# Weight maxima over the partitions through a small tensor in memory instead of TensorE

## The chip, the cores and the metric

The kernel runs on one core of one Trainium2 chip. The metric is the device time of one execution in microseconds, and of several executions the median. The engines are called by the profile's short names in its rows: PE (TensorE), PEld (its weight loads), DVE (the vector engine), ACT (the scalar engine), POOL (GpSimd) and SP (the engine that issues most transfers).

## The reference

A linear attention (RWKV) gives tokens x (3072 × 384). A mixture of 8 experts follows, in which every token goes through every expert, weighted by a matrix that Sinkhorn steps have balanced:

```python
logits = x @ w_gate;  P = np.exp(logits - logits.max())
for _ in range(8):
    P /= P.sum(1, keepdims=True) + 1e-09
    P /= P.sum(0, keepdims=True) + 1e-09
    P *= N / E
for e in range(E):                      # w1: 8 x 384 x 1024, w2: 8 x 1024 x 384
    h = np.maximum(x @ w1[e], 0.0)
    out += P[:, e:e + 1] * (h @ w2[e])
```

All of it is float32. The kernel keeps that accuracy by splitting each float32 operand into a high and a low float16 part and making three float16 matmuls of each product (high by high, high by low, low by high). For the weights this needs a scale: a power of two, found from the largest absolute value of w1 and of w2 in the part at hand. That maximum is over all 128 partitions, and every partition needs it.

## The kernel before, in words

**First part.** The attention runs in 24 chunks, with expert 0's layers interleaved. What is left of expert 0 then runs beside the Sinkhorn steps and the preparation of stage 0's weights.

**Stages.** Experts 1 to 7 are done in 14 stages (`NS`), each half of an expert's hidden dimension (512 of 1024). A stage has 60 slots: two halves of the tokens (g), two column halves (j), and 15 products (n) each. So slots 0 to 14 are g = 0, j = 0; slots 15 to 29 are g = 0, j = 1; slots 30 to 59 are g = 1. In the loop at lines 1135 to 1150 each slot puts out three things, in this order: one product of the first layer (`g1_slots`), three matmuls of 512 columns on TensorE; then the tasks that a table has put on this slot; then 4 or 5 matmuls of 384 columns (5, 5, 5, 5, 4) of the second layer (`g2_tiles`) of the token half before. In stage 0 the token half before belongs to expert 0 and has only a remainder, which is used up in the first half of the 30 slots of g = 0; after it those slots hold first-layer matmuls alone.

**First layer.** A scheme with 15 products in place of 18 computes the layer from sums of weight blocks (made by GpSimd in the preparation) and sums of token blocks. The products go into five chains, each in a PSUM bank of its own: A, Y, Z, C and B (tiles bA, bY, ...). `ORDER` and `CHAIN` (lines 614 to 617) say which product goes on which chain. `after(n)` (line 960) has the vector and the scalar engine read the chains as they grow: `vadd` combines a bank with a temporary in the buffer `tb` (t0, t1, t2, t4, s2), and `keep` makes the two float16 parts of the hidden values, high on the scalar engine, low on the vector engine. A chain's bank is read while the chain is still to be added to, so a later product on it waits for that read; and banks go round, so a new chain waits until the last reader of the bank's old chain is done. Banks come from two pools: every third chain takes one of 2 banks (`ph`), the others one of 4 (`pq`).

**Second layer.** A tile of 128 tokens takes 12 matmuls into one of two PSUM banks (`po`). The scalar engine multiplies by the gate into one of three staging buffers (`stg`), and the tile is added to `accd` in memory, by transfers that GpSimd issues (in stage 0 they are plain stores on SP).

**Preparation of the next stage's weights** (`stage_weights`, line 768; put on slots in `stage_tasks`, line 1088). In slot 0 SP loads raw w1 and w2 into `rawb` (128 × 3072). `amax` (slots 9, 10, 17, 18) takes four column maxima, each over 768 elements a partition, on the vector engine (tiles `wms`). `reduce_max` (slot 19) makes two of them, one for w1 and one for w2 (`wmas`). `across` (slot 21) starts the maximum over the partitions, `over_partitions` (line 134): TensorE transposes the 128 × 2 maxima into a PSUM bank, the vector engine takes the maximum of each row (`mt_s`) and puts the two on the diagonal of a 2 × 2 matrix (`md_s`). `scale` (slot 23) lets TensorE multiply that by ones, which gives both maxima on every partition, and `pow2_scale` (line 126) makes the scale of it in three small operations on the vector engine (`isw` twice, `sw`). The bank for this comes from the pool of 4, after stage 0's own. From slot 30 on the scalar engine (`high`) and the vector engine (`low`) convert the weights by that scale.

**Other tasks.** From stage 2 on, expert 0's results are added in: in slots 8, 23, 38 and 53 SP fetches two pieces (`hb<-e0d`), nine slots later they are summed on the vector engine, then weighted on the scalar engine and added to `accd` by GpSimd. SP takes its transfers in the order in which they were put out and waits at each for what it needs.

Of the kernel before, what the change touches and what calls it, by code (L numbers as in the profile page):

```python
# [8 lines left out]
F32 = mybir.dt.float32  # L9
# [3 lines left out]
ALU = mybir.AluOpType  # L13
AX = mybir.AxisListType
# [18 lines left out]
def rwkv_sinkhorn_moe(  # L33
# [13 lines left out]
    V, S_, G, T, Q = (  # L47
        InOrder(tc, e) for e in (nc.vector, nc.scalar, nc.gpsimd, nc.tensor, nc.sync)
    )
# [3 lines left out]
    E, _, F = w1.shape  # L53
    P = 128
# [6 lines left out]
    TB = 512  # L61
# [10 lines left out]
    sm = ctx.enter_context(tc.tile_pool(name="sm", bufs=2))  # L72
# [41 lines left out]
        return v_[:, :, t % TH, :]  # L114

    accd = dram.tile([NT, DM], F32, name="accd")
    e0d = [dram.tile([NT, DM], F32, name=f"e0d{j}") for j in range(2)]
    logits = const.tile([P, NTT, E], F32, name="logits")
    inv_s = const.tile([P, NTT], F32, name="inv_s")
# [6 lines left out]
    def pow2_scale(m, inv, s, down):  # L126
        V.tensor_scalar(inv, m, 1e-30, down, op0=ALU.max, op1=ALU.mult)
        V.tensor_single_scalar(
            inv.bitcast(I32), inv.bitcast(I32), EXP_MASK, op=ALU.bitwise_and
        )  # L130
        V.reciprocal(s, inv)


    def over_partitions(m, n, pool, tag, name):

        pt = pool.tile([P, TB], F32, tag=tag, name=f"pmax_{name}")
        T.transpose(pt[:n, :P], m, ident)
        mt = sm.tile([P, 1], F32, tag="mt", name=f"mt_{name}")
        V.tensor_reduce(mt[:n], pt[:n, :P], axis=AX.X, op=ALU.max)
        md = sm.tile([P, 2], F32, tag="md", name=f"md_{name}")  # L140
        V.tensor_scalar_mul(md[:n, :n], ident[:n, :n], mt[:n])
        yield pt[:, 2 * P : 2 * P + n]
        T.matmul(pt[:, 2 * P : 2 * P + n], ones[:n, :], md[:n, :n], start=True, stop=True)
        yield pt[:, 2 * P : 2 * P + n]
# [617 lines left out]
    tb_ = big.tile([P, 13 * TS], F32, name="tb")  # L762
# [5 lines left out]
    def stage_weights(s):  # L768
        e, half = 1 + s // 2, s % 2
        home = ws0 if s % 2 == 0 else ws1  # L770
        w1s = part(home, F16, 0, (NPR, 2, TS))
        w2s = part(home, F16, NPR * 2 * TS, (2, FHC, DM))
        isw = sm.tile([P, 2], F32, tag="isw", name=f"isw_{s}", bufs=3)
        sw = sm.tile([P, 2], F32, tag="sw", name=f"sw_{s}")
        m = sm.tile([P, 4], F32, tag="wm", name=f"wms_{s}")
        ma = sm.tile([P, 2], F32, tag="wma", name=f"wmas_{s}")
        uc = part(ucb, F32, 0, (11, TS))

        def load():
            fs = slice(half * FH, (half + 1) * FH)  # L780
            Q.dma_start(raw1, w1[e][:, fs].rearrange("(c p) f -> p c f", p=P))
            Q.dma_start(raw2, w2[e][fs, :].rearrange("(c p) d -> p c d", p=P))

        def amax(i):
            n = KC * FH // 2
            V.tensor_reduce(
                m[:, i : i + 1], rawb[:, i * n : (i + 1) * n],
                axis=AX.X, op=ALU.max, apply_absolute_value=True,
            )

        res = []

        def reduce_max():
            V.tensor_reduce(ma, m.rearrange("p (j i) -> p j i", i=2), axis=AX.X, op=ALU.max)

        def across():
            res.append(over_partitions(ma, 2, *small(), f"s{s}"))
            next(res[0])

        def scale():  # L800
            pow2_scale(next(res[0]), isw, sw, 0.25)

        a = [raw1[:, i % KC, (i // KC) * TS : (i // KC + 1) * TS] for i in range(6)]
        u_ = {r_: uc[:, UI[r_]] for r_ in US[:11]}
        pool = [
            add(u_[0], a[0], a[2]), sub(u_[7], a[3], a[0]), add(u_[1], u_[7], a[4]),
            sub(u_[2], u_[1], a[1]), sub(u_[10], a[2], a[1]), add(u_[3], u_[2], u_[0]),
            sub(u_[8], a[5], u_[10]), add(u_[9], a[3], a[5]), sub(u_[12], a[4], u_[8]),
            sub(u_[13], a[2], a[5]), add(u_[14], a[0], a[5]),
        ]  # L810
        pieces = [
            (w1s[:, i : i + n], uc[:, i : i + n], 0) for i, n in ((0, 3), (3, 3), (6, 3), (9, 2))
        ] + [
            (w1s[:, 11:13], raw1[:, 0:2, :TS], 0), (w1s[:, 13:15], raw1[:, 1:3, TS:], 0)
        ] + [
            (w2s[:, :, i : i + 2].rearrange("p l c d -> p c l d"), raw2[:, i : i + 2], 1) for i in (0, 2)
        ]

        def high(i):
            o, x_, j = pieces[i]  # L820
            S_.activation(o[:, :, 0], x_, AF.Copy, scale=sw[:, j : j + 1])

        def low(i):
            o, x_, j = pieces[i]
            V.scalar_tensor_tensor(
                o[:, :, 1], x_, sw[:, j : j + 1], o[:, :, 0], op0=ALU.mult, op1=ALU.subtract
            )

        return dict(w1s=w1s, w2s=w2s, isw=isw, load=load, amax=amax, reduce_max=reduce_max, across=across,
                    scale=scale, pool=pool, high=high, low=low, n=len(pieces))  # L830

# [38 lines left out]

    def at(t, *fs):
        ticks.setdefault(t, []).extend(fs)

    small_ = [(ps2, "po")]

    def small():
        return small_[0]

    WS = {0: stage_weights(0)}
    sk = sinkhorn()  # L880
# [207 lines left out]
    def stage_tasks(s):  # L1088
        ts = {}

        def at(t, *fs):
            ts.setdefault(t, []).extend(fs)

        def gate():
            pes[s] = gate_of(1 + s // 2, WS[s]["isw"], s)

        at(2, gate)
        if s == 0:
            at(3, gate0)
        if s + 1 < NS:  # L1100
            w_ = WS[s + 1] = stage_weights(s + 1)
            at(0, w_["load"])
            for i, t in enumerate((9, 10, 17, 18)):
                at(t, lambda i=i: w_["amax"](i))
            for i, f in enumerate(w_["pool"]):
                at(8 + i, f)
            at(19, w_["reduce_max"])
            at(21, w_["across"])
            at(23, w_["scale"])
            for i, (th_, tl) in zip(  # L1110
                (4, 6, 0, 7, 1, 5, 2, 3),
                ((0, 2), (1, 3), (8, 9), (8, 10), (15, 17), (16, 18), (23, 24), (23, 25)),
            ):
                at(NSLOT + th_, lambda i=i: w_["high"](i))
                at(NSLOT + tl, lambda i=i: w_["low"](i))
        else:
            for _ in range(2 * FHC):
                at(20, load_final)
        for n in range(4):
            n4 = (s - 2) * 4 + n  # L1120
            if 0 < n4 <= NTT:
                at(15 * n + 2, flush(n4 - 1)[1])
                at(15 * n + 3, flush(n4 - 1)[2])
            if 0 <= n4 < NTT:
                at(15 * n + 8, flush(n4)[0])
        return ts
# [4 lines left out]

    rest = e0_rest()
    late = None
    small_[0] = (ps4, "pq")
    for s in range(NS):
        tasks = stage_tasks(s)
        for g in range(NG):
# [43 lines left out]
```

## Time and profile before

| | |
|---|---|
| median of 3 runs | 1607.49 us (1604.43, 1607.49, 1607.59) |
| the profiled execution's own time | 1602.74 us |
| its span, first to last instruction | 1601.0 us |
| mean granted TensorE clock | 0.995 |
| busy: PE, DVE, ACT, POOL | 98%, 64%, 42%, 37% of the span |
| first layer: one matmul of a chain, 840 each on bY and bZ | mean 379 ns, overlapping |
| second layer: one matmul into po, 3360 with hbx | mean 326 ns, overlapping |

All rows are of one profiled execution. A row of the groups reads: source line, engine, operation, out<-in by the program's names, shapes, count, then the busy time in us and the mean of one in ns, then the idle time of the engine just before and what ended it. A row of the sequence in time reads: start and duration in us, engine, operation, count, and in brackets the idle time before it and its releaser. Most instructions have line 29, a helper's, so tiles tell them apart. Matmuls are pipelined: a matmul's duration holds its way through the array, and the next one starts earlier than it ends.

### The profile page before, as it was taken

The numbers are of one execution on the slowest core, as the hardware profiler recorded it, in microseconds if no ns is written. First come the engines' busy times: TensorE is split into PE (matmuls) and PEld (weight loads), VectorE is DVE, ScalarE is ACT, GpSimd is POOL, SyncE is SP. The second block draws the span as 40 slices with busy tenths as digits, with TensorE's granted clock in tenths as the row PEclk, the third lists the DMA queues.
The fourth block names the chain that finished last, engine by engine and source line by source line (L and its number), as shares of the span: only waits on it lengthen the run. The fifth ranks groups of instructions, "written<-read, shape, count | busy, mean of one in ns | idle before, by whom it ended". The sixth has DMA issues, their size and how long they took to land.

```text
span 1601.0 us, 24304 instructions
## 1 busy us (share of the span) xinstructions
PE 1571.7 (98%) x9433; PEld 909.6 (57%) x9433; DVE 1019.0 (64%) x1706; ACT 668.6 (42%) x1190; POOL 587.9 (37%) x688
## 2 busy tenths in 40 slices
PE   7999999999999999999999999999999999999999
PEld 5778777555455555555555555555555555555555
DVE  6776665675766666666666666666665666656554
ACT  2333333343444444454535454544444453535320
POOL 6567674442021343434243424243332424242200
PEclk8999999999999999999999999999999999999999
DMA  7333230212022567566666656664545554545434
GB/s 180 63 69 85 66 86 26 92 42 84 35 94 54 104 85 124 74 123 85 124 84 100 110 74 123 85 113 55 95 55 94 58 96 54 94 56 89 60 89 133
DMA packets 163899, 136.60 MB, mean 85 GB/s; under 512 B 88257, under 2 KB 158018, under 8 KB 163778
## 3 DMA queue, kind: packets, MB, share of 16 engines
q0 software_dynamic: 44928, 61.36, 31.6%
q1 hardware_dynamic: 118640, 73.63, 15.9%
q8 instruction: 75, 1.23, 0.3%
q14 instruction: 46, 0.38, 0.1%
q10 hardware_dynamic: 210, 0.00, 0.0%
HBM read 53.69 MB, written 80.22 MB: 84 GB/s over the span
## 4 chain that ended last, share of the span: by engine, by line
PE 93%; DVE 3%; POOL 1%; issue 1%; ACT 1%; ACTq 0%; DVEq 0%; POOLq 0%
PE po L29 46%; PE bZ L29 11%; PE bY L29 11%; PE ph L29 5%; PE bB L29 4%; PE bA L29 4%; PE py L29 4%; PE bC L29 2%; PE pA L29 1%; PE pu L29 1%; POOL tb L29 1%; PE pz L29 1%; PE prT L29 1%; PE pkT L29 1%; PE px L29 0%
## 5 line engine op out<-in xcount | busy, mean ns | idle before, releaser
L29 PE MATMUL po<-ws,hbx 128*128 128x384 f16 x3360 | 736.9, 326 | 0.0
L29 POOL DMA_DIRECT2D accd<-stg x288 | 250.4, 870 | 701.2 <-ACT stg L29 682.8
L29 PEld LDWEIGHTS <-hbx 128*128 128x128 f16 x3576 | 336.9, 98 | 287.4
L29 PEld LDWEIGHTS <-ws 128*128 128x128 f16 x3096 | 302.8, 98 | 248.2 <-issue 6.3
L29 ACT ACTIVATE hbx<-tb 128x512 f16<-128x512 f32 x224 | 141.5, 632 | 443.5 <-DVE tb L29 443.5
L29 PE MATMUL po<-ws,hb 128*128 128x384 f16 x1248 | 322.2, 327 | 3.2 <-DVE ws L29 2.3
L29 DVE TENSOR_TENSOR tb<-bY,tb 128x512 f32<-128x512 f32 x168 | 116.2, 692 | 194.4 <-PE bY L29 193.3
L29 ACT ACTIVATE stg<-po,pe 128x384 f32<-128x384 f32 x312 | 179.6, 575 | 128.0 <-PE po L29 102.5
L29 PE MATMUL bZ<-xv,ws 128*128 128x512 f16 x840 | 227.0, 379 | 0.7 <-DVE tb L29 0.6
L29 PE MATMUL bY<-xv,ws 128*128 128x512 f16 x840 | 227.0, 379 | 0.1
L29 DVE TENSOR_TENSOR tb<-bZ,tb 128x512 f32<-128x512 f32 x168 | 115.5, 688 | 132.9 <-PE bZ L29 132.9
L29 PEld LDWEIGHTS <-hb 128*128 128x128 f16 x1248 | 122.1, 98 | 96.4 <-issue 4.7
L29 POOL TENSOR_TENSOR ucb<-rawb 128x256 f32<-128x256 f32 x84 | 75.5, 949 | 93.1 <-DMA rawb<-in_moe_w_dram 66.7
L29 DVE TENSOR_TENSOR tb<-bB,tb 128x512 f32<-128x512 f32 x112 | 77.5, 692 | 49.6 <-PE bB L29 47.7
L29 PE MATMUL ph<-hbx,ws 128*128 128x384 f16 x576 | 103.9, 328 | 1.3 <-DVE hb L29 1.2
L29 DVE SCALAR_TENSOR_TENSOR hbx<-tb,hbx 128x512 f16<-128x512 f32 x112 | 78.0, 696 | 24.3 <-ACT hbx L29 19.5
L29 DVE SCALAR_TENSOR_TENSOR hb<-tb,hbx 128x512 f16<-128x512 f32 x112 | 77.2, 689 | 24.7 <-ACT hbx L29 19.5
L29 PE MATMUL bA<-xv,ws 128*128 128x512 f16 x336 | 90.8, 379 | 1.0 <-ACT tb L29 1.0
L29 PE MATMUL bB<-xv,ws 128*128 128x512 f16 x336 | 90.8, 379 | 0.0
L29 DVE SCALAR_TENSOR_TENSOR hb<-ph,hb 128x384 f16<-128x384 f32 x64 | 35.5, 555 | 59.0 <-ACT hb L29 58.8
L29 ACT COPY tb<-bZ 128x512 f32<-128x512 f32 x56 | 32.8, 586 | 68.1 <-PE bZ L29 68.1
L29 ACT ACTIVATE hb<-ph 128x384 f16<-128x384 f32 x64 | 31.5, 492 | 58.0 <-PE ph L29 56.7
(163 smaller groups left out, 1645.0 us busy)
## 6 DMA issues: line engine op xcount, KB each, us to landing
accd<-stg POOLq DMA_DIRECT2D x288, 192.0 KB, 3.7
rawb<-in_moe_w_dram SPq DMA_DIRECT2D x28, 768.0 KB, 7.3
e0d<-stg SPq DMA_DIRECT2D x48, 192.0 KB, 1.9
hb<-e0d SPq DMA_DIRECT2D x48, 192.0 KB, 3.5
rn<-in_r_dram SPq DMA_DIRECT2D x24, 192.0 KB, 3.1
kn<-in_k_dram SPq DMA_DIRECT2D x24, 192.0 KB, 3.5
vn<-in_v_dram SPq DMA_DIRECT2D x24, 192.0 KB, 2.8
accd<-stg SPq DMA_DIRECT2D x24, 192.0 KB, 1.8
```

Source lines behind the costliest of these rows:

```text
L29: return lambda *a, **k: self.tc.keep_in_program_order(f(*a, **k))
```

## The change

It concerns the maxima over the partitions in the preparations for stages 1 to 13; stage 0's own preparation stays on TensorE. The vector engine's two maxima for each partition (128 × 2) are written to a small tensor in memory, `wmx`, and read back with all 256 values onto every partition, into columns of the buffer `tb` that the stages do not use otherwise. There one reduction on the vector engine gives both maxima, which `pow2_scale` takes as before. The column maxima stand in slots 9, 10, 11 and 15 (before: 9, 10, 17, 18), the two-column maximum and the write in slot 15 (before: 19), the reading back in slot 21, and the reduction with the scale in slot 29 (before: 23).

```diff
+    wmx = dram.tile([2 * E, P, 2], F32, name="wmx")
...
+        mb = tb_[:, 5 * TB : 5 * TB + 2 * P]
 
         def reduce_max():
             V.tensor_reduce(ma, m.rearrange("p (j i) -> p j i", i=2), axis=AX.X, op=ALU.max)
+            if s:
+                Q.dma_start(wmx[s], ma)
 
         def across():
-            res.append(over_partitions(ma, 2, *small(), f"s{s}"))
-            next(res[0])
+            if s:
+                Q.dma_start(
+                    mb, wmx[s].rearrange("(o p) j -> o (p j)", o=1).broadcast_to([P, 2 * P])
+                )
+            else:
+                res.append(over_partitions(ma, 2, ps2, "po", f"s{s}"))
+                next(res[0])
 
         def scale():
-            pow2_scale(next(res[0]), isw, sw, 0.25)
+            if s:
+                mj = sm.tile([P, 2], F32, tag="wmj", name=f"wmj_{s}")
+                V.tensor_reduce(mj, mb.rearrange("p (q j) -> p j q", j=2), axis=AX.X, op=ALU.max)
+            else:
+                mj = next(res[0])
+            pow2_scale(mj, isw, sw, 0.25)
...
-            for i, t in enumerate((9, 10, 17, 18)):
+            for i, t in enumerate((9, 10, 11, 15)):
                 at(t, lambda i=i: w_["amax"](i))
...
-            at(19, w_["reduce_max"])
+            at(15, w_["reduce_max"])
             at(21, w_["across"])
-            at(23, w_["scale"])
+            at(29, w_["scale"])
```

How the instructions move is shown for stage 2, which prepares stage 3's weights.

TensorE in slot 21, before. `bC` is the product of this slot, `pmax_s` the bank of the transpose, `po` the second layer:

```order
L29 MATMUL bC_0_1_9402<-xv_76,ws_74 128x512
L29 LDWEIGHTS ws_74
L29 MATMUL bC_0_1_9402<-xv_76,ws_74 128x512
L29 MATMUL pmax_s_9408<-ident,wmas_9137 2x128
L29 LDWEIGHTS hb_73
L29 MATMUL po_13_9396<-ws_75,hb_73 128x384
L29 LDWEIGHTS hbx
```

And now:

```order
L29 MATMUL bC_0_1_9398<-xv_76,ws_74 128x512
L29 LDWEIGHTS ws_74
L29 MATMUL bC_0_1_9398<-xv_76,ws_74 128x512
L29 LDWEIGHTS hb_73
L29 MATMUL po_13_9392<-ws_75,hb_73 128x384
L29 LDWEIGHTS hbx
```

The transpose is gone, and the second layer follows the first directly. The matmul by ones, after the products of slot 23, is gone in the same way.

The vector engine from slot 14 to slot 19, before. `wms` are the column maxima, `wmas` the two-column maximum, `hb<-hb` the sum of expert 0's pieces, the rows with b and a letter the adds on chains:

```order
L29 TENSOR_TENSOR tb<-bB_0_0_9247,tb 128x512
L29 SCALAR_TENSOR_TENSOR hbx<-bZ_0_0_9162,hbx 128x512
L29 SCALAR_TENSOR_TENSOR hbx<-tb,hbx 128x512
L29 TENSOR_TENSOR tb<-bY_0_1_9337,tb 128x512
L29 TENSOR_REDUCE wms_9136<-rawb 128x1
L29 TENSOR_TENSOR hb_73<-hb_73 128x384
L29 TENSOR_REDUCE wms_9136<-rawb 128x1
L29 TENSOR_TENSOR tb<-bY_0_1_9337,tb 128x512
L29 TENSOR_TENSOR tb<-bA_0_1_9324,tb 128x512
L29 TENSOR_REDUCE wmas_9137<-wms_9136 128x2
```

And now, from slot 11 to slot 16:

```order
L29 TENSOR_TENSOR tb<-bZ_0_0_9157,tb 128x512
L29 TENSOR_TENSOR tb<-bB_0_0_9242,tb 128x512
L29 TENSOR_REDUCE wms_9131<-rawb 128x1
L29 SCALAR_TENSOR_TENSOR hbx<-tb,hbx 128x512
L29 SCALAR_TENSOR_TENSOR hbx<-bY_0_0_9147,hbx 128x512
L29 TENSOR_TENSOR tb<-bB_0_0_9242,tb 128x512
L29 SCALAR_TENSOR_TENSOR hbx<-bZ_0_0_9157,hbx 128x512
L29 SCALAR_TENSOR_TENSOR hbx<-tb,hbx 128x512
L29 TENSOR_REDUCE wms_9131<-rawb 128x1
L29 TENSOR_REDUCE wmas_9132<-wms_9131 128x2
L29 TENSOR_TENSOR tb<-bY_0_1_9336,tb 128x512
```

One column maximum stands behind the two adds of slot 11; the other, with the two-column maximum, stands ahead of slot 16's add on chain Y.

The vector engine in slots 21 to 23, before. `mt_s` and `md_s` are the steps between TensorE's two, `isw` and `sw` the scale:

```order
L29 TENSOR_REDUCE mt_s_9410<-pmax_s_9408 2x1
L29 TENSOR_SCALAR md_s_9412<-ident,mt_s_9410 2x2
L29 TENSOR_TENSOR tb<-bY_0_1_9337,tb 128x512
L29 SCALAR_TENSOR_TENSOR hbx<-tb,hbx 128x512
L29 TENSOR_TENSOR tb<-bZ_0_1_9348,tb 128x512
L29 TENSOR_SCALAR isw_9134<-pmax_s_9408 128x2
L29 TENSOR_SCALAR isw_9134<-isw_9134 128x2
L29 RECIPROCAL sw_9135<-isw_9134 128x2
```

And now the steps stand in slot 29, between the operations of its own chain and the add of slot 31 (last row):

```order
L29 TENSOR_TENSOR tb<-bB_0_1_9435,tb 128x512
L29 SCALAR_TENSOR_TENSOR hbx<-bZ_0_1_9347,hbx 128x512
L29 TENSOR_REDUCE wmj_9497<-tb 128x2
L29 TENSOR_SCALAR isw_9129<-wmj_9497 128x2
L29 TENSOR_SCALAR isw_9129<-isw_9129 128x2
L29 RECIPROCAL sw_9130<-isw_9129 128x2
L29 SCALAR_TENSOR_TENSOR hbx<-tb,hbx 128x512
L29 TENSOR_TENSOR tb<-bY_1_0_9522,tb 128x512
```

`mt_s` and `md_s` have gone; the reduction of the values read back (`wmj`) and the three operations of the scale follow slot 29's adds, ahead of the last low part of that slot. On SP the write and the reading back stand next to each other, between the fetches of slots 8 and 23. On the scalar engine and on GpSimd the order is as before.

More of the change, by code (lines that the diff above doesn't have):

```diff
@@ L872, in at @@
         ticks.setdefault(t, []).extend(fs)
-    small_ = [(ps2, "po")]
-    def small():
-        return small_[0]
     WS = {0: stage_weights(0)}
@@ L1133, in rwkv_sinkhorn_moe @@
     late = None
-    small_[0] = (ps4, "pq")
     for s in range(NS):
```

## The prediction

> **What bounds the kernel now.** I read the head of the page and its chain of waits first, then a table by stretches, then TensorE's own sequence around the step that the change takes off it.
>
> ```profile
> span 1601.0 us, 24304 instructions
> PE 1571.7 (98%) x9433; PEld 909.6 (57%) x9433; DVE 1019.0 (64%) x1706; ACT 668.6 (42%) x1190; POOL 587.9 (37%) x688
> ...
> PE 93%; DVE 3%; POOL 1%; issue 1%; ACT 1%; ACTq 0%; DVEq 0%; POOLq 0%
> ```
>
> TensorE (PE) is busy for 98% of the span and carries 93% of the chain that ended last. But busy time of pipelined matmuls is no proof that an engine never waits, so the stretches come next: for each, the busy time of PE, PEld, DVE, ACT and POOL.
>
> ```profile
> 400.00:484.00 84.00, 81.91 (x437) 42.62 (x437) 57.95 (x91) 36.95 (x66) 8.62 (x11) 1.00 0.18 64
> 484.00:570.00 86.00, 86.00 (x472) 45.98 (x471) 54.56 (x85) 39.24 (x70) 25.39 (x31) 1.00 0.46 79
> 570.00:656.00 86.00, 86.00 (x472) 45.98 (x471) 55.94 (x88) 40.78 (x72) 32.26 (x39) 1.00 0.64 101
> 1432.00:1518.00 86.00, 86.00 (x472) 45.98 (x471) 49.92 (x79) 38.63 (x69) 20.80 (x24) 1.00 0.53 74
> ```
>
> From 484 us to 1518 TensorE has no idle time, at a granted clock of 1.00, in stage after stage (first, second and last shown); the vector engine is at 65% there (55.94 of 86). Whatever leaves TensorE's stream in those stages shortens the span, and whatever the change adds elsewhere is free while it fits between TensorE's due times. Before 484 us TensorE does wait: 2.1 us of the 84 from 400 on.
>
> Now one maximum over partitions in such a stage, on TensorE (start, us, then the instruction):
>
> ```profile
> 484.08 0.81 PE L29 MATMUL bC<-xv,ws 128*128 128x512 f16 x3
> 484.72 0.27 PE L29 MATMUL pmax_s<-ident,wmas 128*2 128x128 f32 x1
> 484.83 0.33 PE L29 MATMUL po<-ws,hb 128*128 128x384 f16 x1
> ...
> 487.11 0.81 PE L29 MATMUL bZ<-xv,ws 128*128 128x512 f16 x3
> 487.85 0.38 PE L29 MATMUL pmax_s<-md_s,ones 2*128 2x2 f32 x2
> 488.16 0.50 PE L29 MATMUL po<-ws,hbx 128*128 128x384 f16 x2
> ...
> 488.98 0.81 PE L29 MATMUL bB<-xv,ws 128*128 128x512 f16 x3
> 489.63 0.33 PE L29 MATMUL po<-ws,hb 128*128 128x384 f16 x1
> ```
>
> Starts, not durations, tell the cost, since durations overlap. Three matmuls of 512 columns with nothing behind them take 489.63 − 488.98 = 0.65 us. With the matmul by ones behind them they take 488.16 − 487.11 = 1.05, so it costs 0.40 us. The transpose costs 484.83 − 484.72 = 0.11.
>
> **The change part by part.**
>
> *TensorE loses the transpose and the matmul by ones in 13 of 14 weight preparations.* The count is in the groups by line:
>
> ```profile
> L29 PE MATMUL pmax_s<-md_s,ones 2*128 2x2 f32 x28 | 5.3, 256 | 0.8 <-DVE md_s L29 0.8
> ```
>
> Two rows for each (the product in float32 is done in two passes), so 14 preparations; the first (for stage 0) keeps its own. Of the 13, twelve lie in stages where TensorE never idles: 12 × (0.40 + 0.11) = **6.1 us**. A page's rule beside it: the Trainium skill, "TensorE: Matmul & The Clock Gate", section "Back-to-back issue gap", gives 134 cycles for 128 columns and about 25 ns for very small ones, an estimate of 0.11 us for the three instructions, and 1.3 us in place of 6.1 for twelve. The rows show 0.51 and have the last word.
>
> *The thirteenth (made in stage 0, for stage 1) stands where TensorE waits for the vector engine:*
>
> ```profile
> 402.25 0.81 PE L29 MATMUL bC<-xv,ws 128*128 128x512 f16 x3
> 404.06 0.27 PE L29 MATMUL pmax_s<-ident,wmas 128*2 128x128 f32 x1 [1.01 <-DVE wmas L29]
> 404.17 0.81 PE L29 MATMUL bY<-xv,ws 128*128 128x512 f16 x3
> 404.82 0.81 PE L29 MATMUL bZ<-xv,ws 128*128 128x512 f16 x3
> 406.42 0.38 PE L29 MATMUL pmax_s<-md_s,ones 2*128 2x2 f32 x2 [0.80 <-DVE md_s L29]
> 406.74 0.82 PE L29 MATMUL bB<-xv,ws 128*128 128x512 f16 x3
> ```
>
> Both stall the in-order matmuls behind them: 404.17 − 402.25 − 0.65 = 1.27 and 406.74 − 404.82 − 0.65 = 1.27, together 2.5. It won't all come back: with the matmuls in groups of 0.65 us and no second layer between them, the vector engine is the slower one in these slots and sets the pace. What leaves it there before slot 30:
>
> ```profile
> 405.85 0.27 DVE L29 TENSOR_REDUCE mt_s<-pmax_s 2x1 f32<-2x128 f32 x1
> 406.15 0.22 DVE L29 TENSOR_SCALAR md_s<-ident,mt_s 2x2 f32<-2x2 f32 x1
> ...
> 408.09 0.14 DVE L29 TENSOR_SCALAR isw<-pmax_s 128x2 f32<-128x2 f32 x1
> 408.26 0.17 DVE L29 TENSOR_SCALAR isw<-isw 128x2 int32<-128x2 int32 x1
> 408.46 0.17 DVE L29 RECIPROCAL sw<-isw 128x2 f32<-128x2 f32 x1
> 409.13 0.69 DVE L29 TENSOR_TENSOR tb<-bZ,tb 128x512 f32<-128x512 f32 x1 [0.50 <-PE bZ L29]
> ```
>
> 0.27 + 0.22 are dropped and 0.14 + 0.17 + 0.17 move behind slot 28, 0.97 in all; the 0.50 idle, for a chain that TensorE was late with, goes too. I take **1.5 us** between two ends: 2.5 if all of TensorE's waiting goes, and −0.9 if one of the column maxima, now in slot 11, lands on the path there (its price is below). The value stands near the vector engine's sum because that engine sets the pace here.
>
> *The vector engine's reordering in the full stages: nothing.* The column maxima move from slots 17 and 18 to 11 and 15. Rows of the groups for the prices, then the vector engine and TensorE in one stage (a slot takes about 86/60 = 1.44 us):
>
> ```profile
> L29 DVE TENSOR_REDUCE wms<-rawb 128x1 f32<-128x768 f32 x56 | 51.0, 942 | 0.0
> L29 DVE TENSOR_REDUCE xm<-x 128x1 f32<-128x384 f32 x24 | 13.3, 553 | 0.8
> L29 DVE TENSOR_REDUCE cs<-pc 128x8 f32<-128x192 f32 x8 | 2.8, 347 | 2.8 <-PE pc L29 2.8
> ```
> ```profile
> 729.97 0.69 DVE L29 TENSOR_TENSOR tb<-bB,tb 128x512 f32<-128x512 f32 x1
> 731.35 0.69 DVE L29 SCALAR_TENSOR_TENSOR hbx<-tb,hbx 128x512 f16<-128x512 f32 x1 [0.70 <-ACT hbx L29]
> ...
> 736.38 0.69 DVE L29 TENSOR_TENSOR tb<-bY,tb 128x512 f32<-128x512 f32 x1 [0.74 <-PE bY L29]
> ...
> 758.31 0.69 DVE L29 TENSOR_TENSOR tb<-bY,tb 128x512 f32<-128x512 f32 x1 [0.75 <-PE bY L29]
> ```
> ```profile
> 739.84 0.81 PE L29 MATMUL bY<-xv,ws 128*128 128x512 f16 x3
> ```
>
> The maximum of slot 11 comes right behind the add at 729.97, where 0.70 is idle: 0.94 − 0.70 = 0.24 late at most. That of slot 15 comes ahead of the add at 736.38, where 0.74 is idle; with the two-column maximum (estimated at 0.15, like other operations of a few elements) the add starts 0.94 + 0.15 − 0.74 ≈ 0.35 later. Who waits for that? The bank it reads is written again at 739.84, and the add ended at 737.07: 2.8 us of slack. If that cover were gone, each 0.94 on the path in 13 stages would cost 12 us. The 0.9 above is this same duration.
>
> *The maximum over 256 read-back values* is a new operation: between 347 ns (192 elements a partition) and 553 (384), taken at 0.42 as nearer to the first. With the three small operations it makes about 1.0 us in slot 29, where the 0.75 idle before the add at 758.31 takes most. That add has the same 2.8 us behind it. The scalar engine's conversions in slot 30, which wait for the last of the three, may start some tenths later. What follows them there:
>
> ```profile
> 759.70 0.59 ACT L29 COPY tb<-bZ 128x512 f32<-128x512 f32 x1 [0.47 <-PE bZ L29]
> ```
>
> 0.47 is idle behind them, so nothing is passed on; without that cover 0.2 in 13 stages would be 2.6 us.
>
> *The two transfers on SP's queue: nothing.* The write waits for the two-column maximum, the read for the write's landing; behind both stand only the fetch of slot 23 and, in stages 0 and 1, stores to `accd`, which come a tile at a time. Neighbours from the list of transfers:
>
> ```profile
> hb<-e0d SPq DMA_DIRECT2D x48, 192.0 KB, 3.5
> ...
> wt<-in_w_dram SPq DMA_DIRECT2D x1, 0.8 KB, 2.0
> ```
>
> The write (1 KB in pieces of 8 bytes) I take at the 2.0 us of the other small transfer (a load in pieces of 4 bytes), the read (128 KB) at 3.5. The maximum is ready at about 736.38 + 0.35 = 736.7 and used one subtraction (0.69) ahead of the idle time before 758.31, at 758.31 − 0.75 − 0.69 = 756.9: 20 us for 5.5.
>
> *Sum:* 6.1 + 1.5 = 7.6 us, 0.47% of the profiled execution's 1602.74 us (span 1601.0), which gives 1595.1. The median of the runs shown lies 4.7 higher, so on that scale 1607.49 − 7.6 = **1599.9 us**. A measurement of this kernel can tell about 0.2% (3.2 us) from no change; the runs themselves lie 0.2% apart.
>
> **The rivals.**
>
> *A: the read comes late (slower).* The vector engine works in order, so a read not yet landed at slot 29 holds up every chain behind it. What speaks for it: no store of this kernel goes in pieces as small as 8 bytes so far, and the longest landing of a transfer into or out of the raw weights' buffer was 10.8 us.
>
> ```profile
> DMA to landing us min/median/max: 1.9/2.8/10.8
> ```
>
> The Trainium skill, "DMA: Bandwidth & Descriptors", section "Specifications", says that pieces under 512 B make the engines read, modify and write; no run here shows what that costs this write. Against: it decides only from 20 + 2.8 ≈ 23 us for both together, and 10.8 twice is 21.6. If each took 12.3 (24.6 in all), TensorE would lose 1.6 us in 13 stages: 1607.49 − 7.6 + 20.8 = 1620.7. Chance 3%.
>
> *B: the small product wasn't what cost (no change).* The 0.40 may be a break in the stream that another instruction pays at that place, with only the transpose's 0.11 saved for each maximum. Then 12 × 0.11 + 1.5 = 2.8 us, 1604.7. The page's rule above speaks for this: by it so small a product needs next to nothing of TensorE. Against: at 488.98 the stream goes from 512 columns on to the second layer without any break, and these are the neighbours that remain. Chance 5%.
>
> *C: a freed stall is replaced.* In the full stages the column maxima in slots 11 and 15, a little late, could make a bank late once a stage. If 0.25 us of it reached TensorE in 13 stages, 3.3 would be given back: gain 4.3, 1603.2, still faster; at 0.94 in each (12.2) the kernel would be 4.6 slower, 1612.1. The 2.8 us of slack speak against both. Chance 5% for the first, 1% for the second.
>
> *D: the program doesn't do it.* The order of instructions shows the transposes gone from TensorE and the two transfers on SP, so only an unseen wait is left. It would have to be one of those above.
>
> **How the numbers follow.** Forecast 86%; A 3%, B 5%, C 5% and 1%. The forecast's own range: gains from 6.1 − 0.9 = 5.2 to 6.1 + 2.5 = 8.6, and the level of the runs from 1602.74 to 1607.59: 1602.74 − 8.6 = 1594.1 to 1607.59 − 5.2 = 1602.4. That alone holds over 8 in 10, so it is the range. Faster: forecast and the first C, 91%, less 3% for a measurement that falls inside the bound, 88%. No change: B and those 3%, 8%. Slower: A and the second C, 4%.
>
> **What would show it.** Right: in the full stages TensorE again idles nowhere, and the distance from one stage's gate to the next falls from 86.2 to about 85.65 us. In stage 0 the waits for wmas and md are gone, and TensorE reaches slot 30 about 1.5 us sooner. The small write lands in 2 to 3 us, the read in 3 to 5, and the vector engine never waits for it. Wrong: idle time of the vector engine released by a DMA ahead of wmj (A), a stage period still near 86.1 (B), or idle time of TensorE in slots 13 to 20 or 30 to 35 released by the vector engine (C). A gain under 5 us, or none in stage 0 beyond the vector engine's share, would contradict my sizes even if the sign is right.

## The result, and the profile after

| | before | after |
|---|---|---|
| median, side by side (4 runs each) | 1606.66 us (1604.43 to 1607.59) | 1596.85 us (1595.52 to 1598.68) |
| ratio after / before | | 0.9942, 95% interval 0.9924 to 0.9959 |
| the profiled execution, its span | 1602.74, 1601.0 us | 1598.68, 1597.0 us |

In this first comparison the kernel became 9.3 us faster by the ratio (0.58%; the interval is 6.6 to 12.2 us). Two later comparisons of the same two kernels, with more runs, gave 6.4 and 6.3 us by the ratio (their medians lie 5.3 and 6.3 apart), and those are nearer to what the traces show. From the head of the page of after:

```profile
PE 1567.8 (98%) x9394; PEld 907.6 (57%) x9394; DVE 1021.9 (64%) x1693; ACT 668.0 (42%) x1190; POOL 586.6 (37%) x688
```

TensorE has 39 matmuls fewer (13 preparations by three) and still carries 93% of the chain that ended last. The table by stretches, columns as before:

```profile
400.00:484.00 84.00, 81.07 (x424) 41.71 (x423) 57.40 (x88) 37.63 (x66) 8.44 (x11) 0.98 0.21 66
484.00:570.00 86.00, 86.00 (x472) 45.90 (x470) 55.18 (x83) 39.41 (x69) 24.23 (x31) 1.00 0.45 78
```

In the full stages TensorE still idles nowhere (the list of waits from 484 to 1518 us is empty for it, before and after), so what left its stream shortened them. The first stretch, around stage 0, is the exception: 81.07 busy where before had 81.91. It cuts stage 0 at different places in the two; over stage 0 itself, from its first product to stage 1's, TensorE idles 3.6 us in both (73.63 − 70.05 and 74.56 − 70.94), so it doesn't wait less there. Its sequence in a full stage, in the slots that held the two small products:

```profile
486.43 0.81 PE L29 MATMUL bC<-xv,ws 128*128 128x512 f16 x3
487.08 0.33 PE L29 MATMUL po<-ws,hb 128*128 128x384 f16 x1
...
489.35 0.81 PE L29 MATMUL bZ<-xv,ws 128*128 128x512 f16 x3
490.00 0.49 PE L29 MATMUL po<-ws,hbx 128*128 128x384 f16 x2
```

Both groups of three now take 0.65 us up to the next matmul (487.08 − 486.43, 490.00 − 489.35), where before they took 0.75 and 1.05 with what stood behind them. The length of a whole stage can be read from TensorE's first product on chain A, in before and then in after:

```profile
540.24 0.81 PE L29 MATMUL bA<-xv,ws 128*128 128x512 f16 x3
...
626.41 0.81 PE L29 MATMUL bA<-xv,ws 128*128 128x512 f16 x3
```
```profile
542.07 0.60 PE L29 MATMUL bA<-xv,ws 128*128 128x512 f16 x2
...
627.72 0.81 PE L29 MATMUL bA<-xv,ws 128*128 128x512 f16 x3
```

86.17 us became 85.65, which is 0.52 a stage; from stage 1 to the start of stage 13 it is 1034.07 against 1027.80, so 6.3 us.

The new steps: the two transfers (KB each, median us from issue to landing), then the vector engine around slot 29 of stage 2:

```profile
tb<-wmx SPq DMA_DIRECT2D x13, 128.0 KB, 4.1
...
wmx<-wmas SPq DMA_DIRECT2D x13, 1.0 KB, 5.7
```
```profile
585.05 0.68 DVE L29 SCALAR_TENSOR_TENSOR hbx<-bZ,hbx 128x512 f16<-128x512 f32 x1
585.65 0.41 DVE L29 TENSOR_REDUCE wmj<-tb 128x2 f32<-128x256 f32 x1
```

The write of 1 KB takes longer than the read of 128 KB. Together that is 9.8 us, and the reduction starts right behind the operation ahead of it, with no wait for a transfer in any of the 13. In this stage the write was issued at 566.20 and the read had landed at 575.91, 9.7 us before it was needed.

### The profile page after: what moved, and what is told of

Its sections match the earlier page's. It is cut to its first block, busy times and chain, and to the rows that moved or that the text cites. A ratio compares the mean times of both kernels' runs of the same rounds, so it can differ in the third digit from the quotient of the medians.

```text
span 1597.0 us, 24269 instructions
## 1 busy us (share of the span) xinstructions
PE 1567.8 (98%) x9394; PEld 907.6 (57%) x9394; DVE 1021.9 (64%) x1693; ACT 668.0 (42%) x1190; POOL 586.6 (37%) x688
## 4 chain that ended last, share of the span: by engine, by line
PE 93%; DVE 3%; POOL 1%; issue 1%; ACT 1%; DMA 0%; ACTq 0%; DVEq 0%; POOLq 0%
PE po L29 46%; PE bY L29 11%; PE bZ L29 11%; PE ph L29 5%; PE bA L29 4%; PE bB L29 4%; PE py L29 4%; PE bC L29 2%; PE pA L29 1%; PE pu L29 1%; POOL tb L29 1%; PE prT L29 1%; PE pz L29 1%; PE pkT L29 1%; PE px L29 0%
```

## The experiments

All kernels in one table. "Start" is TensorE's first first-layer product of stage 0, "stage 0" the time from there to stage 1's, "12 stages" from stage 1 to stage 13, each from one profiled execution. The ratio is to the kernel before, run on the same chip.

| kernel | start | stage 0 | 12 stages | ratio, 95% interval |
|---|---|---|---|---|
| before | 380.4 | 73.6 | 1034.1 | |
| before again | 380.1 | 74.0 | 1034.1 | 1.0000, 0.9990 to 1.0011 |
| after | 381.9 | 74.6 | 1027.8 | 0.9942, 0.9924 to 0.9959 |
| after again | 382.0 | 74.4 | 1027.8 | 0.9960, 0.9945 to 0.9975 |
| after, third time | 383.2 | 73.8 | 1027.8 | 0.9961, 0.9949 to 0.9974 |
| route only | 382.9 | 73.9 | 1027.8 | 0.9952, 0.9937 to 0.9967 |
| slots only | 379.7 | 74.1 | 1034.1 | 1.0009, 0.9998 to 1.0020 |
| late write | 379.7 | 76.3 | 1040.2 | one run, 1610.59 to 1603.91 us |
| product twice | 381.1 | 74.2 | 1036.8 | one run, 1606.65 to 1602.62 us |
| stage 0's maxima ahead | 384.3 | 72.2 | 1027.8 | 0.9978, 0.9968 to 0.9989 |
| first preparation too | 384.5 | 74.8 | 1027.8 | 0.9956, 0.9943 to 0.9969 |
| maxima behind Sinkhorn | 383.0 | 72.2 | 1027.8 | 0.9983, 0.9973 to 0.9994 |
| all ahead | 384.6 | 72.2 | 1027.8 | 0.9973, 0.9961 to 0.9985 |
| later load | 385.2 | 72.6 | 1027.8 | 0.9959, 0.9945 to 0.9973 |

**What the measurement can tell: the kernel before again.** No edit.

> The kernel before, unchanged, against itself: shows what the measurement can tell. Both theories: ratio 1.000, within 0.002. Its profile gives a second sample of stage 0 (73.6 us in the first, from its first product on chain A to stage 1's) and of the twelve full stages (86.17 each). Theory 1 (stage 0 and the attention vary with the granted clock, the full stages don't): full stages 86.17 again, stage 0 and what lies ahead of it off by up to 2 us. Theory 2 (they are as fixed as the full stages): 73.6 within 0.2.

1603.54 against 1603.38 us. The interval is ±0.1%, so about 1.7 us can be told apart with this many runs. The full stages are again 86.17 us, stage 0 is 0.4 longer.

**The change again,** twice: on the same chip as the one above and the two below, and on the chip of the kernel with the later load (the last experiment). No edit.

> The changed kernel, unchanged. Theory 1 (the twelve full stages give 6.3 us, stage 0 gives nothing or loses up to 1 us, and the rest of the first comparison's 9.3 us is spread from run to run): ratio 0.995 to 0.9965, full stages 85.65, stage 0 at 73 to 75 us. Theory 2 (stage 0 does give the forecast 1.5 us or more, and the first profile, with TensorE at half its clock there for 2.6 us, was the odd one): stage 0 at 72.1 or less, ratio 0.994 to 0.995.

> The changed kernel once more, on the same chip and against the same runs of the kernel before as the one with the later load, so that those two can be compared directly. Theory 1 (the gain is the twelve full stages and nothing beside): 6.3 us below the kernel before, ratio 0.9955 to 0.9965. Theory 2 (the 9.3 us of the first comparison are what the change brings): ratio about 0.9942.

6.4 us (0.55 to 0.25%) and 6.3 us (0.51 to 0.26%). Both fit the twelve stages alone; the first comparison's further 3 us did not come back.

**The route without the slots:** the maxima go through memory, but the column maxima and the write keep their old slots.

```diff
-            for i, t in enumerate((9, 10, 11, 15)):
+            for i, t in enumerate((9, 10, 17, 18)):
...
-            at(15, w_["reduce_max"])
+            at(19, w_["reduce_max"])
```

> The route through memory with the column maxima back in slots 9, 10, 17, 18 and the two-column maximum in 19. Theory 1 (TensorE's stream alone sets the full stages): 85.65 a stage, as with the change. In stage 0 the maximum ahead of slot 16's add is gone, so that add is up to 0.9 us earlier and TensorE's stall at slot 19 is 0.2 instead of 1.3: stage 0 about 1 to 2 us shorter than with the change, whole kernel 0 to 2 us faster than it, ratio 0.993 to 0.996. Rival (the slots were moved because the old ones leave too little time for the transfers, 10 us in all): the read lands behind slot 29, the vector engine waits there, and a full stage is longer than 85.65.

**The slots without the route:** the kernel before with the new slots for the column maxima and the two-column maximum, and TensorE's products as they were.

```diff
-            for i, t in enumerate((9, 10, 17, 18)):
+            for i, t in enumerate((9, 10, 11, 15)):
...
-            at(19, w_["reduce_max"])
+            at(15, w_["reduce_max"])
```

> TensorE's route as before, with the column maxima in slots 9, 10, 11, 15 and the two-column maximum in 15. Theory 1: full stages 86.17 as before, since the vector engine's order has no part in them; stage 0 about 1 us longer than before (the maximum ahead of slot 16's add), or up to 1 us shorter as the transpose no longer waits 1.0 us for wmas: ratio 0.9990 to 1.0010. Rival (the slots alone bring part of the 6.3): full stages under 86.0, ratio 0.998 or less.

The route alone has the whole 6.3 us of the full stages (1027.8) and a ratio of 0.9952; the slots alone have none of it (1034.1, 1.0009). So the vector engine's new order costs nothing in the full stages and brings nothing, and the gain is TensorE's stream. With its two products the route also takes one bank a stage out of the round of the pool of 4; TensorE waits for no bank in the full stages before or after, so that has no part in the gain there. Stage 0 did not become 1 to 2 us shorter than with the change, as the first theory expected of the route alone: 73.9 against 73.8 to 74.6.

**How much cover the vector engine has: the write and the read put late.** In after, write in slot 26 and read in slot 27, so that the reduction in slot 29 has to wait.

```diff
-            at(15, w_["reduce_max"])
-            at(21, w_["across"])
+            at(26, w_["reduce_max"])
+            at(27, w_["across"])
```

> The changed kernel with the two-column maximum and the write in slot 26 in place of 15, the reading back in 27; the use stays in slot 29. Write and read take 5.4 and 4.2 us to land in the changed kernel's full stages, so the values come about 5.8 us behind the place where the vector engine wants them, and it waits there. Theory 1 (2.8 us of slack between the vector engine's add and the next matmul on its bank, as forecast): TensorE loses 5.8 - 2.8 = 3.0 us a stage, full stages at about 88.6 us. Theory 2 (no slack: a wait of the in-order vector engine is a wait of TensorE): 91.4. Theory 3 (banks and the second layer hide all of it): 85.65.

Two rows from the lists of waits of this kernel (engine and tile, what it waited for: us in total, times, longest), the second for TensorE from 540 to 1490 us:

```profile
DVE wmj L29 <- DMA tb<-wmx: 49.0, 13, 4.2
```
```profile
PE bY L29 <- DVE tb L29: 9.9, 11, 1.3
```

The vector engine waits 49.0/13 = 3.8 us each time. The full stages become 86.68 us on average against 85.65, so 1.03 of that reaches TensorE, at the product on chain Y that the next add holds up. 3.8 − 1.03 = 2.7 us is the cover, and the prediction had read 2.8 from one pair of rows. The wait was shorter than expected, since here the write landed in a median of 2.8 us. This also sizes rival A: it decides from about 10 us of free time plus 2.7, and the two transfers would have to take 12 to 13 us longer than they did.

**What the small product costs: issued twice.** The kernel before, with a second copy of the matmul by ones into a part of its bank that nobody reads.

```diff
+        T.matmul(pt[:, 3 * P : 3 * P + n], ones[:n, :], md[:n, :n], start=True, stop=True)
```

> The kernel before with the product by ones made twice, the second into an unused place of the same bank (nothing reads it). In the kernel before its two passes start 0.13 us apart, with 0.09 ahead and 0.05 behind them beyond what the neighbours take. Theory 1 (each small pass takes its own 0.13 to 0.15 of TensorE): two more passes, full stages at 86.17 + 0.27 to 0.30 = 86.44 to 86.47. Theory 2 (the 0.40 is a break of the stream between float16 and float32 and the passes themselves are nearly free, 0.03 each): 86.23.

TensorE in this kernel (x4: two products of two passes):

```profile
661.13 0.81 PE L29 MATMUL bZ<-xv,ws 128*128 128x512 f16 x3
661.87 0.60 PE L29 MATMUL pmax_s<-md_s,ones 2*128 2x2 f32 x4
662.40 0.50 PE L29 MATMUL po<-ws,hbx 128*128 128x384 f16 x2
```

A full stage takes 86.40 us, 0.23 more than before. So a pass costs 0.11 to 0.12 us, and of the 0.40 that one product of two passes takes, 0.40 − 0.23 = 0.17 lies at its joins to the float16 stream. The second copy has no joins of its own, which fits its costing less than the first. The size lies nearer to what the first theory expected than to the other's and hits neither. After pays no joins at that place at all, which refutes rival B: the break belonged to the float32 product. The rule that the prediction weighed, the Trainium skill, "TensorE: Matmul & The Clock Gate", section "Back-to-back issue gap", with some 25 ns for the smallest matmuls, does not hold for these float32 ones.

**Stage 0: the vector engine's maxima taken out of it.** In after, the raw weights for stage 1 are loaded before stage 0, and their four column maxima are put ahead of it, among the Sinkhorn steps.

```diff
+    WS[1] = stage_weights(1)
+    at(25, WS[1]["load"])
+    for i, t in enumerate((31, 32, 33, 34)):
+        at(t, lambda i=i: WS[1]["amax"](i))
...
```

> The changed kernel with stage 1's raw weights loaded and their four column maxima taken ahead of stage 0, where the vector engine idles 2.9 us at a time; all else as changed. Theory 1 (the vector engine's work sets TensorE's pace in slots 8 to 29 of stage 0): 4 x 0.86 = 3.4 us leave that stretch, TensorE reaches slot 30 at 28 to 29 us after slot 0 instead of 31.6, stage 0 takes about 71 to 72 us, ratio to the kernel before 0.9935 to 0.9950. Theory 2 (the way round from TensorE over scalar and vector engine back to TensorE sets it, not the amount of work): less than 1 us gained, stage 0 at 73.5 or more.

Stage 0 becomes 72.2 us, 2.0 less than the mean of after's three profiled executions (74.3): the vector engine does set the pace where the maxima stand, and four operations of 0.86 to 0.94 us off it are worth 2 us. But the kernel as a whole gained nothing, 0.9978 with an interval that just overlaps after's, and in its profiled execution stage 0 starts later. TensorE ahead of stage 0 in this kernel:

```profile
367.15 0.56 PE L29 MATMUL pc<-pm,ones 128*128 128x192 f32 x2 [2.58 <-DVE pm L29]
367.55 3.77 PE L29 MATMUL po<-ws,hb 128*128 128x384 f16 x12
```

The last Sinkhorn sum (`pc`) waits 2.58 us for the vector engine, 0.16 in after, and the twelve matmuls behind take 3.77 us in place of 2.12, at a granted clock of 0.54 (from 367.5 to 371.2 us).

**The fourteenth preparation too.** In after, stage 0's own weight maxima also go through memory, into a buffer of their own.

```diff
-        mb = tb_[:, 5 * TB : 5 * TB + 2 * P]
+        mb = tb_[:, 5 * TB : 5 * TB + 2 * P] if s else mb0
...
-            if s:
-                Q.dma_start(wmx[s], ma)
+            Q.dma_start(wmx[s], ma)
...
```

> The changed kernel with stage 0's own maxima through memory as well, read back into a buffer of their own. In the kernel before, TensorE waits 3.4 us there for the two-column maximum, runs 17 matmuls at half the clock behind it (2.7 us) and waits 0.8 us more ahead of the product. Theory 1 (these are TensorE's own losses): stage 0 starts 3 to 6 us sooner than in the changed kernel (377 us instead of 382), ratio 0.993 or less. Theory 2 (the Sinkhorn steps and GpSimd's token sums, which the chain of waits shows from 342 to 358 us, set the start of stage 0): less than 1 us sooner, the stalls come back ahead of Sinkhorn's sums, ratio 0.995 to 0.997.

TensorE's waits between 300 and 384 us, first of after, then of this kernel:

```profile
PE pmax_s L29 <- DVE wmas L29: 3.2, 1, 3.2
PE pc L29 <- DVE pm L29: 2.7, 3, 2.0
```
```profile
PE pc L29 <- DVE pm L29: 6.0, 5, 2.3
PE po L29 <- DVE hb L29: 2.5, 1, 2.5
```

The wait of 3.2 us for the maxima goes, and 3.3 + 2.5 come in its place: the same matmuls now wait for the Sinkhorn steps and for hidden values. Removing a wait of TensorE where another engine is late only moves it. 0.9956 is no better than after's 0.9960 and 0.9961 by more than the intervals.

**Stage 0's maxima behind the Sinkhorn steps.** As two experiments above, but in ticks 37 to 40 (the edit against that kernel):

```diff
-    for i, t in enumerate((31, 32, 33, 34)):
+    for i, t in enumerate((37, 38, 39, 40)):
```

> As the run with stage 1's maxima ahead of stage 0, but behind the last Sinkhorn step, so that they no longer hold up its sums (there TensorE stalled 2.7 us more and ran 10 matmuls at half the clock, 1.6 us). Theory 1 (the work of the vector engine sets TensorE's pace in slots 8 to 29 of stage 0): stage 0 again at 72.2, nothing lost ahead of it (its start at 380 to 382.5), whole kernel 2 us faster than the change: ratio 0.9935 to 0.9955. Theory 2 (work moved ahead of stage 0 always costs there what it saves): start of stage 0 later by 2 us, ratio 0.996 to 0.998.

Stage 0 stays at 72.2, and 0.9983 is no better. The vector engine and GpSimd in the last Sinkhorn step but one of this kernel, then TensorE's wait in the last:

```profile
361.09 1.53 POOL L29 TENSOR_TENSOR ucb<-ucb,rawb 128x256 f32<-128x256 f32 x2
...
361.61 0.35 DVE L29 TENSOR_REDUCE cs<-pc 128x8 f32<-128x192 f32 x1
362.00 0.65 DVE L29 TENSOR_SCALAR cs<-cs 128x8 f32<-128x8 f32 x1
...
362.58 0.72 POOL L29 TENSOR_TENSOR ucb<-rawb 128x256 f32<-128x256 f32 x1
362.68 0.20 DVE L29 RECIPROCAL cs<-cs 128x8 f32<-128x8 f32 x1
362.92 0.60 DVE L29 TENSOR_TENSOR pm<-pm,cs 128x192 f32<-128x192 f32 x1
...
363.44 1.74 DVE L29 TENSOR_TENSOR xv<-tb,xv 128x1024 f16<-128x1024 f32 x1
...
367.49 0.56 PE L29 MATMUL pc<-pm,ones 128*128 128x192 f32 x2 [1.90 <-DVE pm L29]
```

The maxima are gone from this step, yet three of its operations are slower than with the later load, below, and TensorE waits 1.90 us for the next sum, 0.16 in after. The early load lets GpSimd begin its sums of weight blocks (`ucb`, from `rawb`) here. That gave a theory: it is GpSimd beside it that slows the vector engine.

**The scale ahead too.** As the one above (the edit is against it), and the two-column maximum with its write also ahead of stage 0, the read in slot 0 and the scale in slot 6.

```diff
+    at(40, WS[1]["reduce_max"])
...
-            at(21, w_["across"])
-            at(29, w_["scale"])
+            at(21 if s else 0, w_["across"])
+            at(29 if s else 6, w_["scale"])
```

> As the run before, with stage 1's two-column maximum and write ahead of stage 0 as well and its scale in slot 6. Theory 1 (only work ahead of the last wait for TensorE's chain Y, slot 25, counts; the scale lay in idle time or behind it): at most 0.2 us better than with the maxima alone, stage 0 at 72.0 to 72.3. Theory 2 (all the vector engine's work up to slot 30 counts alike): the 0.15 of the two-column maximum and 1.0 of the scale both come off, stage 0 at 71.1.

Stage 0 is 72.16 against 72.21: about 1.1 us of vector work moved away (0.41, three times 0.17, and 0.16 for the two-column maximum) changes nothing. Of this work only the column maxima were on the path.

**The load behind the Sinkhorn steps,** so that GpSimd can't begin early.

```diff
-    at(25, WS[1]["load"])
+    at(34, WS[1]["load"])
```

> The four maxima of the first weight stage's successor stand ahead of stage 0 as in the kernel that put them behind the Sinkhorn steps, and the load of those weights is put nine ticks later, so that GpSimd's sums over them can't begin while VectorE is in its Sinkhorn steps. Theory 1, that the early sums beside those steps were what that kernel lost ahead of stage 0: the pause of TensorE before the product into pc falls from 2.07 back to about 0.3 us, VectorE's cs returns from 0.65 to about 0.17 us, stage 0 starts at 380 to 382.5 us, stage 0 stays 72.2 us long, and the ratio to the kernel before is 0.9935 to 0.9955. Theory 2, that any VectorE work that is put ahead of stage 0 costs there what stage 0 saves: stage 0 starts at 383 us or later and the ratio stays at 0.996 to 0.998.

The same step in this kernel:

```profile
365.55 0.35 DVE L29 TENSOR_REDUCE cs<-pc 128x8 f32<-128x192 f32 x1
365.93 0.17 DVE L29 TENSOR_SCALAR cs<-cs 128x8 f32<-128x8 f32 x1
366.13 0.20 DVE L29 RECIPROCAL cs<-cs 128x8 f32<-128x8 f32 x1
366.37 0.36 DVE L29 TENSOR_TENSOR pm<-pm,cs 128x192 f32<-128x192 f32 x1
366.65 1.22 DVE L29 TENSOR_TENSOR xv<-tb,xv 128x1024 f16<-128x1024 f32 x1
...
369.68 0.56 PE L29 MATMUL pc<-pm,ones 128*128 128x192 f32 x2 [0.16 <-DVE pm L29]
```

The operations are back at 0.17, 0.36 and 1.22, and TensorE's wait is 0.16 where it was 1.90. So the mechanism of the first theory is shown. Its time isn't: 0.9959 against after's 0.9961 on the same chip, no gain, and a start at 385.2 where the theory had 380 to 382.5 and after (third time) has 383.2. These 2.0 us arise at stage 0's own maxima. TensorE there, in this kernel and in after (third time):

```profile
324.04 0.27 PE L29 MATMUL pmax_s<-ident,wmas 128*2 128x128 f32 x1 [4.28 <-DVE wmas L29]
...
330.01 0.59 PE L29 MATMUL pc<-pm,ones 128*128 128x192 f32 x2 [0.61 <-ACT stg L29]
```
```profile
323.70 0.27 PE L29 MATMUL pmax_s<-ident,wmas 128*2 128x128 f32 x1 [3.21 <-DVE wmas L29]
...
328.00 0.59 PE L29 MATMUL pc<-pm,ones 128*128 128x192 f32 x2 [0.61 <-ACT stg L29]
```

The wait for the maxima is longer, but the transpose behind it starts only 0.34 us later. The rest lies between it and the next sum (`pc`): 330.01 − 324.04 = 5.97 us here and 328.00 − 323.70 = 4.30 there. TensorE had a granted clock of 0.56 from 324.1 to 328.0 in this execution, and of 1.00 in the other. Neither needs the moved maxima: the kernel with the product twice, which moves none, waits 4.27 there, and the profiled executions of before and after take 5.98 and 5.97 up to the sum. So stage 0 is 1.2 us shorter than in after beside it (72.6 against 73.8), and the later start of this one execution says nothing against it; but a gain of that size is below what the comparison can tell (±0.14%, 2.2 us). No version here was shown to beat the changed kernel.

## Why the prediction was right, and where it wasn't

**The full stages: right.** 12 × 0.51 = 6.1 us was forecast; 12 × 0.52 = 6.3 came, in every kernel with this route and free transfers. Starts in place of durations gave the price, and the doubled product confirmed that it belongs to the product.

**The vector engine's order, the reduction, the cover: right.** No wait of TensorE in the full stages; the reduction took 0.41 us (0.42 estimated); the cover is 2.7 (2.8).

**The transfers: the conclusion right, a size wrong.** The read took 4.1 us (3.5 assumed), the write 5.7 (2.0, and "lands in 2 to 3 us" among the signs). The neighbour row was a load in small pieces into the chip's own memory; the write goes the other way, and no row of before had its like. 20 us of room hid the error.

**Stage 0: wrong.** The failed step is "The thirteenth (made in stage 0, for stage 1) stands where TensorE waits for the vector engine", with 1.5 us taken between 2.5 and −0.9, since "that engine sets the pace here". Stage 0 became no shorter: means of 73.8 us in before's two profiled executions and 74.3 in the three of after, 73.9 with the old slots. By the prediction's own signs, that contradicts its sizes. Executions of one kernel lie up to 0.7 apart, mostly by slots 0 to 14 and once by a stretch at half the clock (the last section); sharper is the part from the product on A in slot 15 to the first matmul of the second layer in slot 30. In before and in the repeat of after:

```profile
400.10 0.81 PE L29 MATMUL bA<-xv,ws 128*128 128x512 f16 x3 [0.97 <-ACT tb L29]
...
411.89 0.33 PE L29 MATMUL po<-ws,hbx 128*128 128x384 f16 x1
```
```profile
402.26 0.81 PE L29 MATMUL bA<-xv,ws 128*128 128x512 f16 x3 [1.04 <-ACT tb L29]
404.18 0.81 PE L29 MATMUL bY<-xv,ws 128*128 128x512 f16 x3 [1.11 <-DVE tb L29]
...
414.22 0.98 PE L29 MATMUL po<-ws,hbx 128*128 128x384 f16 x5
```

It is 11.79 us before, 11.56 with the route alone (414.64 − 403.08), 12.20 with the slots alone (411.59 − 399.39) and 11.96 with both (11.95 in after's third execution). So the route gave 0.2, the slots took 0.4, and 0.2 was lost where 1.5 had been forecast. The waits for the maxima (1.0 and 0.8 us) are gone, but TensorE's waits for the vector engine's reads of chains (tb) rose from 0.6 us in stage 0 to 2.5 in after and 3.9 in the repeat. Two errors of the working stand behind it.

First, the sum of 0.97 counted operations that cost nothing, and the 0.50 us of idle time as part of the gain. The vector engine with the route alone, at the place of the scale operations, then TensorE there:

```profile
410.22 0.68 DVE L29 TENSOR_TENSOR tb<-bZ,tb 128x512 f32<-128x512 f32 x1
411.88 0.69 DVE L29 TENSOR_TENSOR tb<-bZ,tb 128x512 f32<-128x512 f32 x1 [0.97 <-PE bZ L29]
```
```profile
410.96 0.81 PE L29 MATMUL bZ<-xv,ws 128*128 128x512 f16 x3 [0.58 <-DVE tb L29]
```

The idle time grew from 0.50 to 0.97, by the 0.48 of the three operations that left. In this place neither engine is the slower one. The work goes round between them: the vector engine reads chain Z, TensorE's next product on it has waited for that read (0.58), and the vector engine waits for that product (0.97). Operations inside such a loop's waits are filling, and taking them out only lets the wait be seen. Of the 1.47 us that the working let go (0.97 + 0.50), the route alone gained 0.23. The bank that the route takes out of the round may have a part in that; it was not separated.

Second, the prediction put the changed slots of the column maxima only into the lower bound, and there named the maximum of slot 11; the one that cost was that of slot 15. The vector engine in the repeat of after:

```profile
402.38 0.94 DVE L29 TENSOR_REDUCE wms<-rawb 128x1 f32<-128x768 f32 x1
403.36 0.16 DVE L29 TENSOR_REDUCE wmas<-wms 128x2 f32<-128x4 f32 x1
403.43 0.69 DVE L29 TENSOR_TENSOR tb<-bY,tb 128x512 f32<-128x512 f32 x1
```

The maximum of slot 15 stands ahead of the add on chain Y, the product that follows on Y (404.18) waits 1.11 us for it, and in before that product started 0.85 us behind the one on A, with no wait of this size. So where a wait for the maxima went, a wait for the add came, in a place that has no second layer to fill it. That is the mechanism of rival C, which had looked for it in the full stages; it came in this stage alone.

**The total.** By the traces 6.3 − 0.2 = 6.1 us; two comparisons say 6.3 and 6.4, the first 9.3. The forecast of 7.6 held since its failed term was small beside the twelve stages; that it lies between those figures is luck, since its 1.5 us for stage 0 never came and the first comparison's further 3 us are not in the traces. The two profiled spans differ by less, 4.1 us, because in that execution of after stage 0 starts 1.4 us later and is 0.9 longer. Ahead of it the diff changes nothing; the start spreads from 379.7 to 381.1 in four kernels with TensorE's route and from 379.7 to 383.2 in five with the other. It goes with the granted clock (seventh column) of an early stretch: 379.7 to 380.4 where that was 1.00, 381.1 and 381.9 where it was 0.92, 382.0 to 383.2 where it was 0.76. Before and after (third time):

```profile
79.00:100.00 21.00, 18.70 (x161) 14.71 (x157) 14.08 (x24) 8.20 (x16) 10.57 (x9) 1.00 0.25 55
```
```profile
79.00:100.00 21.00, 18.72 (x127) 14.94 (x126) 12.65 (x22) 7.12 (x13) 7.86 (x7) 0.76 0.25 54
```

Whether the later start is chance or belongs to the changed program can't be said from so few executions; whatever it is, the timed comparisons contain it.

## What to carry to other kernels

Price an instruction on the bounding engine by the starts of its neighbours, with and without it, and count it only in stages where that engine never waits: there the sum was right to 0.2 us of 6.3. Where two engines wait for each other in turn, removed or moved work turns into waiting; follow the loop once round and ask what each step waits for next, before a saving is booked. A round trip through memory is a cheap replacement for a small product on TensorE if some 10 us of free time lie between, and every operation put ahead of an in-order engine's next due one has to be looked for in the emptiest stage as well as in the fullest.

## What the runs showed of the hardware

**The vector engine beside GpSimd.** With GpSimd's sums running, single operations of the vector engine went from 0.17 to 0.65, 0.36 to 0.60 and 1.22 to 1.74 us, while the reduction and the reciprocal beside them stayed at 0.35 and 0.20. In the kernel with the later load, where they take the shorter times, GpSimd has no operation from 363.6 to 373.9 us. The Trainium skill, "SBUF — State Buffer", section "Who interferes with whom", says that operations with two inputs in SBUF, and tensor-by-scalar operations in the faster modes, share a port pair with GpSimd that one of them holds for a whole instruction, and that reductions never do. The rows agree on which operations are slowed and which aren't; whether the tensor-by-scalar one ran in a faster mode, no row shows.

**A small store.** 1 KB in pieces of 8 bytes took a median of 5.7 us to land in after, 4.0 from the old slot 19 and 2.8 from slot 26. What makes it depend on its place was not tried.

**The clock after short pauses.** In the profiled execution of after, two pauses of 1.04 and 1.11 us were followed by a stretch at half the clock (granted 0.50 from 404.8 to 406.1 us):

```profile
401.65 0.81 PE L29 MATMUL bA<-xv,ws 128*128 128x512 f16 x3 [1.04 <-ACT tb L29]
403.57 1.44 PE L29 MATMUL bY<-xv,ws 128*128 128x512 f16 x3 [1.11 <-DVE tb L29]
404.81 1.49 PE L29 MATMUL bZ<-xv,ws 128*128 128x512 f16 x3
```

The products start 1.24 us apart in place of 0.65. Up to the first matmul of the second layer this execution needs 414.24 − 401.65 = 12.59 us, 0.63 more than the repeat; the rest of the slower stretch went where the repeat waits for the vector engine. In both repeats the same two pauses had no such effect (404.18, then 404.82 in the first). So in one of this kernel's three profiled executions a stretch at half the clock came on top of the pauses; what decides it the runs don't show.
